# Batch 1's attention scores from float32 q and k as loaded, in a kernel of top-32 attention and two gated layers

## The chip, the cores and the metric

The kernel runs on one core of one Trainium2 chip. The metric is the device time of one execution in microseconds. Engine names in the profile: PE is TensorE's matmul, PEld its weight load, DVE is VectorE, ACT is ScalarE, POOL is GpSimd, SP is the engine from whose queue most DMAs are issued.

## The reference, cut to what matters

Three layers follow one another. The change lies in the first.

```python
# q, k, v: (4, 8, 576, 64) float32: 4 batches, 8 heads, 576 positions, 64 dims
scores = (1.0 / np.sqrt(D)) * np.matmul(q, k.transpose(0, 1, 3, 2))
kth = np.partition(scores, -32, axis=-1)[..., -32:-31]
scores = np.where(scores >= kth, scores, -1000000000.0)   # keep the 32 largest
attn = softmax(scores)
x = np.matmul(attn, v)                                    # -> (2304, 512)
x = (sigmoid(x @ w_gate) * (x @ w_val)) @ w_out           # d_ff 1536
# then: a noisy top-2 router over 8 experts, relu(x @ w1[e]) @ w2[e], weighted sum
```

Which 32 scores of a row are kept depends on their order, so the scores need more than float16's precision.

## The kernel before, in words

**Units.** Attention is cut into units of one batch `b`, one pair of heads `hp` (4 pairs) and one block of 128 query rows. 576 rows are four full blocks and one of 64 rows. A full unit has two tiles, one per head, of 128 queries by 576 keys; a half unit holds the 64 rows of both heads in one tile. So a batch has 16 full units with 32 tiles, and 4 half units with 4 tiles. q and k come transposed, with the two heads of a pair on rows (partitions) 0 to 63 and 64 to 127.

**Where q and k come from.** `kq_ops` (from L200) has two ways. With `first` true, k and q of a pair are loaded as float32 into a "khl" buffer (L213, L214), and the score matmul reads them there. With `first` false they are loaded into a staging tile "st" (L224, L225); ACT copies them times 64 to float16 (L235), POOL scales the original by 64 (L236) and subtracts the float16 part from it (L237), which leaves the low half; then SP copies the halves in eight strips into "khl" and "qs" (L232, L233), so that each head has its high and low half one above the other on 128 rows. Before, batch 0 goes the first way, batches 1 to 3 the second. There are 5 "khl" buffers and 3 "st" buffers; a pair of the second way takes two "st" while it is split, and keeps one until its strips are laid. The weights of the second layer pass through the same "st" buffers, ahead of these pairs.

**The score matmuls.** `qk` in `attention` has the same two ways. For batch 0, a tile is two float32 matmuls (288 keys each) on the 64 rows of its head (L336). For the others a tile is four float16 matmuls on all 128 rows, with high and low half of q against k's high halves, then k's low halves (L344); a half unit's are eight, on 64 columns of the array each (L347). One PSUM tile "ps" takes the scores; ACT copies it to SBUF (L352) before the next tile may be written. The scale of the exponent (`SC`) and a factor that the cut-off search uses (`facs`) differ between the two ways, since the second way's scores are 64 x 64 times as large.

**After the scores.** DVE finds each row's largest values (L361 to L370), ACT and POOL a lower bound of the cut-off (L396 to L402), DVE the exact cut-off (L409) and the mask (L424); ACT takes the exponent (L379). PE transposes the masked rows (L453 to L473), ACT copies them out (L460 to L480), and PE multiplies them with v (L494). The transposes, the product with v and the router's steps share three PSUM banks "tp". The products become the input of the second layer, `moe1` (L534, L573), which runs on PE by chunks of 128 or 256 rows whenever a chunk is ready; its end holds the router (its logits are read by DVE at L637, L638). The experts (L804, L830) come last.

**What sets the order.** Each operation is given to a small planner (`Plan`) with an engine, a duration as an estimate, a priority and the buffers that it takes. The planner plays the schedule through and emits the instructions of every engine in the order in which they start there. On the chip each engine's queue is in that order. Attention's priority is ten times the unit's number; the loads of a batch's q and k have that of its units less 70. Operations of one engine that take the same kind of buffer keep the order in which they were made. A score operation is told to take 0.9 us in batch 0 and 0.5 us in the others.

Of the kernel before, what the change touches and what calls it, by code (L numbers as in the profile page):

```python
# [17 lines left out]
OP = mybir.AluOpType  # L18
PSUM = bass.MemoryType.PSUM

B, H, S, D = 4, 8, 576, 64
# [7 lines left out]
SQ, SX, SG, SV, SO, SX2, S1, S2 = 2.0 ** 6, 2.0 ** 6, 2.0 ** 4, 2.0 ** 5, 2.0 ** 6, 2.0 ** 7, 2.0 ** 6, 2.0 ** 6  # L29
# [4 lines left out]

CUT = 1.75 + 2.0 ** -23, 1.75

SC = [1.0 / 8.0] + [1.0 / (8.0 * SQ * SQ)] * (B - 1)
SW = S + 8
TILES = B * 36
LOD = 4, 1  # L40
# [8 lines left out]
class Plan:  # L49
# [10 lines left out]
    def op(self, eng, dur, prio, fn, deps=(), alloc=(), use=(), lat=None, chain="", dma=False):  # L60
        o = Unit()
        o.eng, o.dur, o.prio, o.fn, o.lat = eng, dur, prio, fn, LAT[eng] if lat is None else lat
        o.alloc, o.use, o.next, o.same = list(alloc), list(alloc) + list(use), [], []
        o.n, o.id, o.dma = 0, len(self.ops), dma
        deps = list(deps)
        for t in {h.tag for h in o.alloc}:
            deps.append(self.last.get((eng, chain, t)))
            self.last[eng, chain, t] = o
        for d in deps:
            if d is not None:  # L70
                (d.same if d.eng == eng and not d.dma else d.next).append(o)
                o.n += 1
        for h in o.use:
            h.left += 1
        self.ops.append(o)
        return o
# [51 lines left out]
def attention_moe_kernel(ctx: ExitStack, tc: tile.TileContext, qT, kT, v, w_gate, w_val, w_out,  # L128
# [3 lines left out]
    V, A, P, G = nc.vector, nc.scalar, nc.tensor, nc.gpsimd  # L132
# [25 lines left out]
    facs = const.tile([128, 2, 2], FT, name="facs")  # L158
    G.memset(facs, CUT[1])
    for b in range(2):  # L160
        G.memset(facs[:, b, 0:1], -SC[b])
    NB = (REG - CAP) // BLK
    nbi = const.tile([1, E + 2], I32, name="nbi")
    ohsum = const.tile([128, E], FH, name="ohsum")
# [15 lines left out]
    def layers(fast):  # L180
# [12 lines left out]
        op = plan.op  # L193

        def tile_of(tag, shape, dt, name=None):
            pool = psum if tag in ("ps", "tp", "mm") else stage if tag == "st" else work
            return pool.tile(shape, dt, name=name or tag, bufs=CAPS[tag])
# [112 lines left out]
        def attention(u, kqr, prio):  # L310
# [16 lines left out]
            for t in R:  # L327
                hp_ = plan.tile("ps")

                def qk(t=t):  # L330
                    T[t].ps = tile_of("ps", [128, 2, 512], FT)
                    if u.b == 0:
                        for j in range(2):
                            for s in (t,) if u.nt == 2 else range(2):
                                d = slice(64 * s, 64 * s + 64)
                                P.matmul(T[t].ps[:, j, :288] if u.nt == 2 else T[t].ps[d, j, :288], kqr.kq[d, 1, u.q0:u.q0 + n],  # L336
                                         kqr.kq[d, 0, j * 288:j * 288 + 288], start=True, stop=True)
                        return
                    for c in range(2):
                        for j in range(2):  # L340
                            o = T[t].ps[:, j, :288]
                            ks = slice(j * 288, (j + 1) * 288)
                            if u.nt == 2:
                                P.matmul(o, kqr.qs[:, t, u.q0:u.q0 + 128], kqr.khl[:, c, t, ks], start=c == 0, stop=c == 1)  # L344
                            else:
                                for s in range(2):
                                    P.matmul(T[t].ps[64 * s:64 * s + 64, j, :288], kqr.qs[:, s, 512:576],  # L347
                                             kqr.khl[:, c, s, ks], start=c == 0, stop=c == 1)

                def cp(t=t):  # L350
                    T[t].s = tile_of("sS", [128, S], FT)
                    A.activation(T[t].s.rearrange("p (j n) -> p j n", j=2), T[t].ps[:, :, :288], AF.Copy)  # L352
                a = op("PE", 0.5 if u.b else 0.9, prio, qk, kqr.done, alloc=[hp_], use=[kqr.h])
                cps.append(op("ACT", 0.54, prio, cp, [a], alloc=[T[t].hs], use=[hp_]))

            def chunks(t):
# [7 lines left out]
            def top(rounds, src, tmp, first):  # L364
# [6 lines left out]
                if not fast:  # L371
                    for t in R:
                        V.tensor_copy(good[:, TILES + 6 - u.i - t:TILES + 7 - u.i - t], T[t].m[:, 31:32])
                    V.tensor_scalar(u.m[:, :, 32], u.m[:, :, 0], -SC[u.b], None, op0=OP.mult)

            def ex(t):
                def f():
                    T[t].e = tile_of("e", [128, S], FT)
                    A.activation(T[t].e, T[t].s, AF.Exp, bias=T[t].m[:, CM:CM + 1], scale=SC[u.b])  # L379
                return f  # L380

            if fast:
                c1 = []
                for t in R:
                    c1.append(op("DVE", 1.16, prio, chunks(t), c1 + [cps[t]], alloc=[] if t else [u.hm], use=[T[t].hs]))
                c2 = op("DVE", 1.62 if u.nt == 2 else 1.45, prio, lambda: top(3, lambda t: T[t].cand, lambda t: T[t].cand, 0), c1)
                c2 = op("POOL", 0.15, prio - 1, lambda: G.tensor_tensor(  # L387
                    u.m[:, :, 24:26], u.m[:, :, 0:24:23], facs[:, min(u.b, 1), None, :].to_broadcast([128, u.nt, 2]), op=OP.mult),
                    [c2], use=[u.hm])
                ys = []  # L390
                for t in R:
                    hg = plan.tile("sg")

                    def sg(t=t):
                        T[t].sg = tile_of("sg", [128, S], BF)
                        A.activation(T[t].sg, T[t].s, AF.Sign, scale=-CUT[0], bias=T[t].m[:, 25:26],  # L396
                                     accum_out=T[t].m[:, 26:27])

                    def y(t=t):
                        T[t].y = tile_of("y", [128, SW], FT)  # L400
                        G.tensor_scalar(T[t].y[:, S:], places, T[t].m[:, 26:27], NEG, op0=OP.add, op1=OP.mult)
                        G.tensor_tensor(T[t].y[:, :S], T[t].s, T[t].sg, op=OP.mult)  # L402
                    a = op("ACT", 0.78, prio, sg, [c2], alloc=[hg], use=[T[t].hs])
                    ys.append(op("POOL", 1.4, prio, y, [a], alloc=[T[t].hy], use=[hg, T[t].hs]))
                exs = [op("ACT", 0.68, prio + 0.5, ex(t), [c2], alloc=[T[t].he], use=[T[t].hs]) for t in R]

                def rank():
                    for t in R:
                        V.max(good[:, TILES - 1 - u.i - t:TILES + 7 - u.i - t], T[t].y)  # L409
                r4 = op("DVE", 0.68 * u.nt, prio, rank, ys + ranks[-1:], use=[T[t].hy for t in R])  # L410
            else:
                def whole():
                    alloc_m()
                    for t in R:
                        T[t].y = tile_of("y", [128, SW], FT)[:, :S]
                    top(4, lambda t: T[t].s, lambda t: T[t].y, 0)
                r4 = op("DVE", 4.9 * u.nt, prio, whole, cps, alloc=[u.hm] + [T[t].hy for t in R], use=[T[t].hs for t in R])
                exs = [op("ACT", 0.68, prio + 0.5, ex(t), [r4], alloc=[T[t].he], use=[T[t].hs]) for t in R]
# [43 lines left out]
            for t in R:  # L462
                ht = plan.tile("tp")
                a = op("PE", 0.44, prio, tr(t), [mk[t], ch.open], alloc=[ht], use=[T[t].he])
                evs.append(op("ACT", 0.5, prio, ev(t), [a] + evs[-1:], alloc=[hpt] if t == 0 else [],
                              use=[ht] + ([hpt] if t else [])))
# [7 lines left out]
            a = op("PE", 0.11 * u.nt + 0.11, prio, tr5, mk + [iv, ch.open], alloc=[h5], use=[T[t].he for t in R] + [hpx])  # L474
# [13 lines left out]
            def av():  # L488
                u.po = tile_of("tp", [128, n], FT)
                for kb in range(NK):  # L490
# [5 lines left out]
            a = op("PE", 1.31 if u.nt == 2 else 0.78, prio, av, evs + [VB[u.b, kb][2] for kb in range(NK)],  # L496
                   alloc=[hav], use=[hpt] + [VB[u.b, kb][0] for kb in range(NK)])
# [10 lines left out]
            a = op("DVE", 0.22, prio - 1, times, [a], use=[hav, hpx])  # L508
# [379 lines left out]
        i = 0  # L888
        for b in range(B):
# [3 lines left out]
            for qt in range(5) if b < B - 1 else (4, 0, 1, 2, 3):  # L893
# [11 lines left out]
                for hp in range(4):  # L905
                    u = Unit()
# [6 lines left out]
        KQ = {(0, 0): kq_ops(0, 0, -10, True)}  # L913
# [27 lines left out]
        if fast:  # L941
            a = op("SP", 5.0, 26, load_small)
# [18 lines left out]
        late = [r for u in [u for u in units if u.ends][-2:] for r in u.ch.rows]  # L961
        for i, u in enumerate(units):
            if (u.b, u.hp) not in KQ:
                KQ[u.b, u.hp] = kq_ops(u.b, u.hp, 10 * i - 70, False)
            if (u.b, 0) not in VB:
                for kb in range(NK):
                    v_ops(u.b, kb, 10 * i - 20)
            attention(u, KQ[u.b, u.hp], 10 * i)
            if (u.b, u.q0, u.hp) == (1, 128, 0):
                init_out(10 * i)  # L970
            if u.ends:
                moe1(u.ch, 10 * i + PM)
                if len(routers) == ends - 2:
                    raise_counts(0, 512)
                    early = list(entered)
# [83 lines left out]
```

## Time and profile before

| | us |
|---|---|
| median of 3 runs | 1325.57 (1324.25 to 1325.79) |
| the profiled execution | 1323.6 |
| its span, first to last instruction | 1321.9 |
| PE busy | 1228.2 |
| DVE busy | 869.1 |
| ACT busy | 791.6 |
| POOL busy | 740.9 |

The mean granted TensorE clock is 0.955 of full speed. Batch 1's scores are the matmuls of L344 and L347 between 246 and 415 us of the span.

Busy time is the union of an engine's instructions, and matmuls overlap in it: one may start before the one ahead has left the array. What a group of matmuls takes of PE's time is read from its start to the start of what follows it without a wait.

### The profile page before, as it was taken

Reading aid. Unit: us, or ns where it says so; the run is one execution under the profiler, and the core shown is the slowest. Engines: PE = TensorE matmul, PEld = TensorE weight load, DVE = VectorE, ACT = ScalarE, POOL = GpSimd, SP = SyncE. Lnnn points to the kernel's source line nnn. Section 1 sums busy time; section 2 is a strip of 40 time slices with the busy share of each in tenths; the row PEclk is TensorE's granted clock in tenths of the full one; section 3 lists DMA queues with packets and bytes.
Section 4 is the critical chain, followed back from the end, with each engine's and each line's share of the span. In section 5 each row is a group of like instructions: output and inputs, shape, how many; then the busy total and the mean of one; then the engine's idle time right before and its main releaser. Section 6 shows DMA issues by size and latency. Waiting matters only on the chain. (4 is left out here: it accounts for less than half of the span.)

```text
span 1321.9 us, 29643 instructions
## 1 busy us (share of the span) xinstructions
PE 1228.2 (93%) x10669; PEld 896.4 (68%) x10670; DVE 869.1 (66%) x3608; ACT 791.6 (60%) x1788; POOL 740.9 (56%) x1005
## 2 busy tenths in 40 slices
PE   5578799799999999999999999999999999999997
PEld 3347466586776867886777876877666666676674
DVE  6999889998799887888789875455114324233111
ACT  5777678787777877786787774565224324333221
POOL 5989887787476786666676654442222322222221
PEclk9558899899999899999999999999999999999999
DMA  7434331342004310014100003167547576575441
GB/s 222 115 108 122 124 106 27 100 133 112 17 2 101 87 47 10 11 36 121 53 2 2 18 9 97 50 185 204 99 73 194 122 159 171 102 189 132 77 72 22
DMA packets 104463, 119.93 MB, mean 91 GB/s; under 512 B 56561, under 2 KB 65905, under 8 KB 104306
## 3 DMA queue, kind: packets, MB, share of 16 engines
q1 hardware_dynamic: 94194, 97.97, 27.1%
q0 software_dynamic: 10112, 19.97, 8.2%
q8 instruction: 86, 1.41, 0.5%
q14 instruction: 71, 0.58, 0.2%
HBM read 77.22 MB, written 20.63 MB: 74 GB/s over the span
## 5 line engine op out<-in xcount | busy, mean ns | idle before, releaser
L534 PEld LDWEIGHTS <-w 128*128 128x128 f16 x3456 | 276.9, 100 | 38.0 <-issue 12.9
L534 PE MATMUL mm<-xch,w 128*128 128x256 f16 (+1 forms) x2880 | 285.9, 256 | 7.4 <-ACT th L541 3.7
L812 DVE SCALAR_TENSOR_TENSOR g<-mm,g 128x256 f16<-128x256 f32 (+1 forms) x192 | 72.0, 379 | 243.6 <-ACT g L809 233.1
L402 POOL TENSOR_TENSOR y<-sS,sg 128x576 f32<-128x576 f32 x144 | 194.9, 1354 | 9.1
L804 PE MATMUL mm<-xch,w 128*128 128x256 f16 (+1 forms) x2016 | 190.3, 255 | 0.0
L804 PEld LDWEIGHTS <-w 128*128 128x128 f16 x2016 | 170.2, 98 | 23.5
L361 DVE MAX8 cand<-sS 128x8 f32<-128x72 f32 x1152 | 166.8, 217 | 20.6 <-ACT sS L352 20.2
L830 PEld LDWEIGHTS <-g 128*128 128x128 f16 x960 | 92.8, 98 | 106.3 <-DVE g L812 3.4
L573 PE MATMUL mm<-w,g 128*128 128x512 f16 x648 | 158.2, 389 | 1.0 <-POOL w L281 0.7
L424 DVE SCALAR_TENSOR_TENSOR e<-sS,good,e 128x576 f32<-128x576 f32 x144 | 155.5, 1099 | 2.3 <-ACT e L379 1.5
L786 POOL DMA_INDIRECT v<-xd,ids x40 | 47.0, 1175 | 163.5 <-DVE ws L776 155.1
L842 POOL DMA_INDIRECT out<-e,ids x40 | 63.8, 1595 | 131.3 <-ACT e L839 58.6
L809 ACT ACTIVATE g<-mm 128x256 f16<-128x256 f32 (+1 forms) x192 | 65.8, 346 | 112.6 <-PE mm L804 106.6
L551 POOL TENSOR_TENSOR g<-th,g 128x128 f16<-128x128 f32 (+1 forms) x144 | 93.5, 653 | 68.8 <-ACT g L548 65.7
L409 DVE MAX8 good<-y 128x8 f32<-128x584 f32 x144 | 109.9, 763 | 25.8 <-POOL y L402 21.0
L396 ACT ACTIVATE sg<-sS,m 128x576 bf16<-128x576 f32 x144 | 110.7, 770 | 23.5 <-POOL m L387 22.6
L494 PE MATMUL tp<-pt,v 128*64 128x128 f32 (+3 forms) x1600 | 116.9, 285 | 7.0 <-ACT e L379 5.1
L830 PE MATMUL tp<-w,g 128*128 128x512 f16 x504 | 115.6, 379 | 1.7 <-DVE g L812 1.6
L494 PEld LDWEIGHTS tp<-pt,v 128*64 128x64 f32 (+1 forms) x1600 | 85.2, 143 | 41.5 <-issue 23.5
L573 PEld LDWEIGHTS <-g 128*128 128x128 f16 x648 | 63.6, 100 | 67.6 <-issue 9.2
L453 PE MATMUL tp<-ident,e 128*128 128x128 f32 x576 | 91.6, 296 | 17.2 <-DVE e L424 15.7
L379 ACT ACTIVATE e<-sS,m 128x576 f32<-128x576 f32 x144 | 106.5, 768 | 0.2
(160 smaller groups left out, 2073.7 us busy)
## 6 DMA issues: line engine op xcount, KB each, us to landing
st<-w SPq DMA_DIRECT2D x64, 512.0 KB
khl<-st SPq DMA_DIRECT2D x48, 144.0 KB
st<-w_gate SPq DMA_DIRECT2D x12, 512.0 KB
st<-w_val SPq DMA_DIRECT2D x12, 512.0 KB
st<-w_out SPq DMA_DIRECT2D x12, 512.0 KB
out<-x SPq DMA_DIRECT2D x6, 768.0 KB
v<-v_s SPq DMA_DIRECT2D x16, 256.0 KB
xd<-y SPq DMA_DIRECT2D x16, 256.0 KB
```

The lines of the kernel that those rows point to most:

```text
L361: V.max(T[t].cand[:, 8 * c:8 * c + 8], T[t].s[:, 72 * c:72 * c + 72])
L379: A.activation(T[t].e, T[t].s, AF.Exp, bias=T[t].m[:, CM:CM + 1], scale=SC[u.b])
L396: A.activation(T[t].sg, T[t].s, AF.Sign, scale=-CUT[0], bias=T[t].m[:, 25:26], accum_out=T[t].m[:, 26:27])
L402: G.tensor_tensor(T[t].y[:, :S], T[t].s, T[t].sg, op=OP.mult)
L409: V.max(good[:, TILES - 1 - u.i - t:TILES + 7 - u.i - t], T[t].y)
L424: return lambda: V.scalar_tensor_tensor(T[t].e, T[t].s, good[:, TILES + 6 - u.i - t:TILES + 7 - u.i - t], T[t].e, op0=OP.is_ge, op1=OP.mul ...
L494: P.matmul(u.po[64 * s:64 * s + 64, :], VB[u.b, kb][1][:k, (2 * u.hp + s) * D:(2 * u.hp + s + 1) * D], rhs, start=kb == 0, stop=kb == NK - 1)
L534: P.matmul(r.ps[:, a, :], wt.t[:, a, c, kb, fo:fo + 128], ch.x[x][:, kb, :], start=i == 0, stop=i == 11)
L551: G.tensor_tensor(r.g[:, 1], r.th, r.g[:, 0], op=OP.subtract)
L573: P.matmul(r.ps, g[:, c, 128 * t:128 * t + 128], WO[f // 4].t[:, d, f % 4, :], start=f == 0 and i == 0, stop=f == 11 and i == 2)
L804: P.matmul(r.ps, W[kb].w[c][:, 0, f * 128:f * 128 + 128], q.x[:, 4 * x + kb, :], start=i == 0, stop=i == 11)
L830: P.matmul(r.ps, gs[f].g[:, c, 128 * t:128 * t + 128], W[4 + f // 2].w[d][:, f % 2, :], start=f == 0 and i == 0, stop=f == 7 and i == 2)
```

## The change

Batch 1's scores go the first way, as batch 0's: q and k are loaded as float32 and used as they are. Batches 2 and 3 stay as they were. The scale and the factor follow, and so does the planner's estimate.

```diff
-SC = [1.0 / 8.0] + [1.0 / (8.0 * SQ * SQ)] * (B - 1)
+SC = [1.0 / 8.0] * 2 + [1.0 / (8.0 * SQ * SQ)] * 2
...
     for b in range(2):
-        G.memset(facs[:, b, 0:1], -SC[b])
+        G.memset(facs[:, b, 0:1], -SC[2 * b])
...
-                    if u.b == 0:
+                    if u.b < 2:
                         for j in range(2):
...
-                a = op("PE", 0.5 if u.b else 0.9, prio, qk, kqr.done, alloc=[hp_], use=[kqr.h])
+                a = op("PE", 0.5 if u.b > 1 else 0.9, prio, qk, kqr.done, alloc=[hp_], use=[kqr.h])
...
-                    u.m[:, :, 24:26], u.m[:, :, 0:24:23], facs[:, min(u.b, 1), None, :].to_broadcast([128, u.nt, 2]), op=OP.mult),
+                    u.m[:, :, 24:26], u.m[:, :, 0:24:23], facs[:, u.b // 2, None, :].to_broadcast([128, u.nt, 2]), op=OP.mult),
...
-                KQ[u.b, u.hp] = kq_ops(u.b, u.hp, 10 * i - 70, False)
+                KQ[u.b, u.hp] = kq_ops(u.b, u.hp, 10 * i - 70, u.b < 2)
```

## Rows read from the trace of the kernel before

**Rows 1.** The page's busy times: engine, busy us, share, instructions.
```profile
PE 1228.2 (93%) x10669; PEld 896.4 (68%) x10670; DVE 869.1 (66%) x3608; ACT 791.6 (60%) x1788; POOL 740.9 (56%) x1005
```

**Rows 2.** Busy us (instructions) by stretch; granted clock, DMA share, GB/s last.
```profile
0.00:100.00 100.00, 63.39 (x222) 37.44 (x224) 85.75 (x297) 67.34 (x132) 79.54 (x104) 0.70 0.49 147
...
180.00:260.00 80.00, 66.90 (x583) 47.60 (x584) 72.78 (x337) 62.15 (x140) 61.38 (x90) 0.89 0.29 76
260.00:440.00 180.00, 172.11 (x1511) 130.92 (x1509) 159.15 (x766) 137.13 (x317) 131.92 (x203) 0.98 0.25 76
440.00:820.00 380.00, 372.64 (x3650) 289.83 (x3649) 315.99 (x1574) 282.71 (x678) 253.85 (x405) 1.00 0.14 40
```

**Rows 3.** Instructions on tile ps: count, ns min/median/max, first and last start.
```profile
L344 PE MATMUL ps<-khl,qs x384: 282/286/444, 246.2 to 788.4; 128*128 128x288 f16 x192
...
L336 PE MATMUL ps<-khl x160: 402/507/847, 4.5 to 243.4; 64*128 64x288 f32 x128, 64*64 64x288 f32 x32
...
L347 PE MATMUL ps<-khl,qs x96: 286/286/310, 401.6 to 630.9; 128*64 128x288 f16 x96
```

**Rows 4.** PE's timeline around float32 scores: start, length, line, operands, count.
```profile
211.19 1.23 PE L336 MATMUL ps<-khl 64*128 64x288 f32 x4
212.36 1.51 PE L534 MATMUL mm<-xch,w 128*128 128x128 f16 x24
...
216.38 0.38 PE L473 MATMUL tp<-ident,e 128*64 128x128 f32 x2
216.69 1.23 PE L336 MATMUL ps<-khl 64*128 64x288 f32 x4
```

**Rows 5.** PE's timeline around float16 scores.
```profile
285.89 0.65 PE L344 MATMUL ps<-khl,qs 128*128 128x288 f16 x4
286.38 2.78 PE L534 MATMUL mm<-xch,w 128*128 128x256 f16 x24
...
293.81 0.38 PE L473 MATMUL tp<-ident,e 128*64 128x128 f32 x2
294.03 1.47 PE L534 MATMUL mm<-xch,w 128*128 128x256 f16 x12
```

**Rows 6.** PE's timeline at a float32 half unit of batch 0.
```profile
225.43 1.19 PE L336 MATMUL ps<-khl 64*64 64x288 f32 x8 [1.07 <-ACT sS L352]
226.55 1.46 PE L494 MATMUL tp<-pt,v 128*64 128x128 f32 x20
```

**Rows 7.** PE's timeline at the last float16 half unit of batch 1.
```profile
414.09 0.68 PE L347 MATMUL ps<-khl,qs 128*64 128x288 f16 x8
414.71 1.48 PE L534 MATMUL mm<-xch,w 128*128 128x256 f16 x12
```

**Rows 8.** POOL's subtraction for the halves: count, ns min/median/max, first and last start.
```profile
L237 POOL TENSOR_TENSOR st<-st x12: 2361/2378/2936, 183.3 to 604.2; 128x1152 f16<-128x1152 f32 x12
```

**Rows 9.** POOL's timeline, one of these subtractions.
```profile
230.43 2.37 POOL L237 TENSOR_TENSOR st<-st 128x1152 f16<-128x1152 f32 x1
```

**Rows 10.** DVE's timeline beside it.
```profile
230.49 2.92 DVE L424 SCALAR_TENSOR_TENSOR e<-sS,good,e 128x576 f32<-128x576 f32 x1
...
236.43 0.16 DVE L638 TENSOR_TENSOR sp<-sp,tp 128x8 f32<-128x8 f32 x1
```

**Rows 11.** The masks on DVE: count, ns min/median/max, first and last start.
```profile
L424 DVE SCALAR_TENSOR_TENSOR e<-sS,good,e x144: 798/819/2918, 20.7 to 834.0; 128x576 f32<-128x576 f32 x144
```

**Rows 12.** PE's timeline, the next matmul after that: in brackets the wait.
```profile
236.74 2.60 PE L494 MATMUL tp<-pt,v 128*64 128x128 f32 x20 [5.13 <-ACT e L379]
```

**Rows 13.** ACT's last copy ahead of that matmul, in the timeline of all engines.
```profile
232.95 0.26 ACT L480 ACTIVATE px<-tp 128x128 f32<-128x128 f32 x1
```

**Rows 14.** PE's busy us and granted clock in a stretch.
```profile
234.00:240.00 6.00, 3.26 (x24) 0.50 0.66 151
```

**Rows 15.** PE's waits behind the first and the third score group of batch 1.
```profile
249.12 0.33 PE L471 MATMUL tp<-ident,px 128*128 128x128 f32 x1 [2.27 <-DVE cand L370]
...
253.19 0.33 PE L471 MATMUL tp<-ident,px 128*128 128x128 f32 x1 [0.57 <-POOL px L443]
```

## Prediction

> **What bounds the kernel now.** I read the page's busy times first, then a table of busy time by stage, then the PE timeline of the two kinds of score matmul, then the waits and the DVE and POOL timelines around the largest PE stall. The page says that PE is busy for 93% of the span [rows 1]. The table says where it is not [rows 2]: in the first 100 us PE works 63.39 us, in 180 to 260 us (the end of batch 0's attention and the start of batch 1's) 66.90 of 80, in 260 to 440 us 172.11 of 180, in 440 to 820 us 372.64 of 380. So before about 260 us the attention steps on DVE (72.78 of 80 busy) set the pace and PE has holes; after it PE is the bound. What is not done in a hole is done later, so the end moves by what PE's work grows, less what its holes shrink.
>
> **Where the change falls.** Only batch 1 changes. Its scores ran from 246 us [rows 3] to 415 us [rows 7]: nearly all in the stage in which PE is the bound. That decides the sign for me.
>
> **Scores on PE, full tiles.** A full unit has two score tiles (one per head). Before, a tile is four float16 matmuls on all 128 rows; 384 of them stand for batches 1 to 3 [rows 3], so batch 1 has 128, or 32 tiles. After, a tile is two float32 matmuls, which the trace of batch 0 shows as four instructions on 64 rows. From the start of a group of four to the start of what follows without a wait:
> - float32: 212.36 - 211.19 = 1.17 us [rows 4];
> - float16: 286.38 - 285.89 = 0.49 us [rows 5].
> That is 0.68 us more. The entry costs too: after the pair of L473 the float32 group starts 216.69 - 216.38 = 0.31 us later [rows 4], a 128-row matmul 294.03 - 293.81 = 0.22 us later [rows 5]: 0.09 us. So 0.77 us a tile, and 32 x 0.77 = 24.6 us.
>
> The bounds: within a float32 group the four starts are closer than the group is long. Its 1.23 us [rows 4] hold three steps and one duration; with the median duration of 0.51 us [rows 3] a step is 0.24 us and four are 0.96, that is 0.47 over float16: 32 x 0.47 = 15.0 us if the edges of the group were hidden. I take 0.77, because it is what the rows show to the instruction behind; 15.0 and 24.6 are the ends.
> The rule that bears on this stands in the Trainium skill, "TensorEngine Tiling (Array Packing)", section "Key Properties": changing the tiling mode, not just the tile, drains TensorE. By that rule the edges can't be hidden, since the neighbours are 128-row matmuls, and the trace agrees (1.17 against 0.96); it gives 24.6, without it the sum would be 15.0.
>
> **Scores on PE, the half tiles.** The last 64 rows of batch 1 have four units. Before, eight float16 matmuls on 64 columns (96 for three batches [rows 3]): 414.71 - 414.09 = 0.62 us [rows 7]. After, eight float32 instructions on 64x64: 226.55 - 225.43 = 1.12 us [rows 6]. Four x 0.50 = 2.0 us. Both change the mode at the edges. PE's work grows by 24.6 + 2.0 = 26.6 us (17.0 at the low end).
>
> **What is removed.** For each of batch 1's four head pairs: an ACT copy to float16, a POOL scaling, a POOL subtraction of 2.38 us [rows 8], eight strip copies on SP's queue and the staging tiles. POOL's own time is worth nothing: no PE wait is on it. But DVE pays for the subtraction. At 230.43 it starts and takes 2.37 us [rows 9]; the mask on DVE that starts at 230.49 takes 2.92 us [rows 10] where its median is 0.82 [rows 11]: 2.1 us lost. The Trainium skill, "SBUF — State Buffer", section "Who interferes with whom", calls this an exclusive lock between DVE and GpSimd, and holds it for the whole instruction; the trace agrees for this mask, which ends 0.6 us behind the subtraction.
>
> Here that loss reached PE. PE waits 5.13 us once, from 231.6 to 236.7 us [rows 12]; the row names ACT, but the last of ACT's copies that this step reads had ended at 233.2 [rows 13]. The attention-times-v step writes a PSUM bank of the three that the router's logits also use, and DVE reads those last at 236.43 [rows 10], in order behind the slow mask. And PE's clock was granted at 0.50, the 1.2 GHz level, in 234 to 240 us [rows 14], after PE had stood still. If batch 1's subtraction is not there, 2.1 us of the wait go. Of the 6 us at the low level half was lost (3.0 us); I count half of that again, 1.5 us, as not certain. After the stall goes, the next in line are the router's own DVE steps.
>
> I don't count four such gains. The splits of batch 2 are chained behind batch 1's for the staging tiles "st" alone, so they move up: two of them (three tiles, two per pair in work, one held until its strips are laid) take the places that batch 1's first two had, and the third runs when the first is laid. What is fewer is some three splits in 225 to 300 us, and behind 260 us DVE is not what PE waits for: all PE idle of 260 to 440 us is 7.9 us [rows 2].
>
> **What the holes swallow.** The first batch 1 scores fall where PE waits anyway: 2.27 us behind the first and 0.57 us behind the third [rows 15]. The longer tiles fill 0.77 + 0.57 = 1.3 us of it, unless what PE waits for starts later for them.
>
> **Moved.** Pair 0 of batch 1 finds the fifth "khl" buffer free and is loaded at the start instead of at 170 us: two DMAs, 0.59 MB. At the 147 GB/s of that stage [rows 2] this is 4.0 us of DMA time, and the weight loads queued behind it on SP are late by up to that. DVE, which is busy 85.75 of the first 100 us, hides it: 0, at most 4.0. The other three pairs' loads wait on SP for a buffer of batch 0, as their strips did before, with two DMAs behind the wait instead of eight; the x writes and v loads queued behind it on SP gain, and PE waits for neither: 0. New factors, scales and their index: same instructions, 0. The planner is told 0.9 instead of 0.5 us, so the queues' order changes; that is a gain or a loss for which no row stands, and I bound it by one stall like the one above: 5.1 + 3.0 = 8.1 us either way, taken as 0.
>
> **Sum.** 26.6 - 2.1 - 1.5 - 1.3 = +21.7 us. On the profiled execution's 1323.6 us (span 1321.9 and 1.7 around it) that gives 1345.3; the median of the runs shown lies 2.0 us above that execution, so **1347**.
>
> **Rivals.**
> - **A, faster: DVE is freed and all holes close.** Place: 180 to 440 us. Idle there is 13.1 + 7.9 = 21.0 us [rows 2]. The granted clock of 0.89 over 80 us means 17.6 us at the low level, half lost, 8.8; 0.98 over 180 us likewise 3.6. Together 33.4 us: 26.6 - 33.4 = -6.8, 1319. It decides from 26.6 us recovered on. For it: the one stall shown hangs on a split. Against it: three splits of batch 2 run in the same stretch, and only that stall (6.6 us with its clock) has this cause in the rows.
> - **B, no change: the two heads run side by side.** They lie on rows 0 to 63 and 64 to 127. If they overlapped, two tiles would take 1.26 against 0.98 us: 16 x 0.28 = 4.5, + 2.0 - 4.9 = +1.6, 1327. The Trainium skill's same section says that tiles run matmuls in parallel. Against it: there is one score tile in PSUM, so head 1 waits for ACT's copy of head 0, and the rows show groups of four with other work between them [rows 4].
> - **C, worse: the new order makes another stall** of 8.1 us and the old one stays (3.6 us back): 1347 + 11.7 = 1359. For it: 0.4 us a tile is what the planner believes, 0.77 is what PE takes, so PE runs late on its plan.
> - **D, cheaper tiles:** 17.0 - 4.9 = +12.1, 1338.
>
> **Chances.** Forecast 0.66 (its own range 1339 to 1356), C 0.15, D 0.05, A 0.09, B 0.05. About 0.2% (2.7 us) is what a measurement of this kernel can tell from no change. Slower: forecast, C and D, 0.86; same: B, 0.05; faster: A, 0.09. The range leaves out A, B and the far part of C: 1330 to 1359.
>
> **What would show it.** In the changed trace: L336 with twice its instructions and 1.17 us to the next start; PE busy up by about 20 to 27 us; PE idle of 260 to 440 us still under 10 us; eight L237 instead of twelve; the 5.1 us stall shorter or gone. It is wrong if PE's busy time hardly grows, or if PE's idle time in 180 to 440 us falls from 21 us to under 5.

## The result, and the profile after

| | kernel before | changed kernel | ratio, 95% interval |
|---|---|---|---|
| first comparison | 1325.21 us | 1341.97 us (1337.91 to 1345.53) | 1.0126 (1.0089 to 1.0163) |
| second comparison (run a1_again) | 1324.10 us | 1337.93 us (1335.70 to 1341.85) | 1.0113 (1.0093 to 1.0134) |

The change makes the kernel slower: by 16.8 and 13.8 us between the medians, by 17 and 15 us by the ratios, whose intervals run from 12 to 22 us. 1347 was forecast, with 1330 to 1359 as the range. The profiled execution is the first comparison's slowest, 1345.53 us; the sum that started from the profiled execution before gave 1345.3.

The page of the changed kernel, to be read beside [rows 1]: PE's busy time rose by 22.0 us, and the span by 21.9. (In the profiled execution of a1_again, which is the same kernel, PE's busy time is 1242.1 us, 13.9 above the kernel before, and the span is 1334.0; the last section comes back to this.)

```profile
span 1343.8 us, 29515 instructions
...
PE 1250.2 (93%) x10669; PEld 902.4 (67%) x10670; DVE 862.4 (64%) x3608; ACT 789.6 (59%) x1784; POOL 728.4 (54%) x997
```

PE's idle time as a whole is the same, 93.6 against 93.7 us, but it lies elsewhere. The same table of stages as [rows 2] (PE, PEld, DVE, ACT, POOL busy, granted clock, DMA share, GB/s), first a row of the kernel before that [rows 2] leaves out, then the changed kernel's:

```profile
100.00:180.00 80.00, 64.56 (x595) 47.15 (x593) 70.34 (x216) 57.09 (x133) 72.57 (x81) 0.85 0.37 116
...
100.00:180.00 80.00, 61.64 (x545) 44.95 (x544) 73.17 (x224) 60.34 (x136) 77.93 (x82) 0.81 0.34 112
180.00:260.00 80.00, 72.55 (x603) 50.27 (x601) 72.14 (x353) 61.99 (x144) 58.40 (x93) 0.91 0.19 56
260.00:440.00 180.00, 178.66 (x1453) 128.84 (x1451) 147.32 (x734) 128.59 (x304) 112.84 (x189) 1.00 0.19 59
440.00:820.00 380.00, 367.90 (x3582) 286.60 (x3581) 312.74 (x1564) 279.99 (x670) 249.52 (x396) 1.00 0.13 36
```

In 180 to 440 us PE idles 7.5 + 1.3 = 8.8 us where it idled 21.0; in 260 to 440 us it has almost no room left. DVE does less there (147.32 against 159.15 us of 180). In 100 to 180 us PE idles 18.4 us against 15.4, in 440 to 820 us 12.1 against 7.4. (The stretches are cut by time, so they don't hold the same work in both kernels.) ACT's copies of the scores now wait for PE, as the page's group of L352 shows (busy, mean ns of one, idle ahead of it and what ended most of that). They wait 26.4 us for L336 and 9.3 for L344; before, it was 12.4 and 3.7:

```profile
L352 ACT ACTIVATE sS<-ps 128x576 f32<-128x576 f32 x144 | 92.9, 645 | 36.0 <-PE ps L336 26.4
```

PE's timeline around three score groups of batch 1, to be read beside [rows 4 and 5]:

```profile
305.26 1.24 PE L336 MATMUL ps<-khl 64*128 64x288 f32 x4
306.42 1.09 PE L453 MATMUL tp<-ident,e 128*128 128x128 f32 x8
307.35 1.47 PE L534 MATMUL mm<-xch,w 128*128 128x256 f16 x12
308.76 1.23 PE L336 MATMUL ps<-khl 64*128 64x288 f32 x4
...
405.01 1.19 PE L336 MATMUL ps<-khl 64*64 64x288 f32 x8
406.13 1.48 PE L534 MATMUL mm<-xch,w 128*128 128x256 f16 x12
```

A full tile takes 306.42 - 305.26 = 1.16 us to the next start, a half unit 1.12. The entry shows too: twelve matmuls of L534 take 308.76 - 307.35 = 1.41 us ahead of a score group. In the kernel before, the same twelve take 295.34 - 294.03 = 1.31 us ahead of a float16 group ([rows 5] has their start):

```profile
295.34 0.65 PE L344 MATMUL ps<-khl,qs 128*128 128x288 f16 x4
```

The large stall is gone. POOL's subtractions are eight instead of twelve, and in 225 to 260 us there is none. DVE's masks at that place take 0.80 us, about their median, and DVE reads the router's logits at 234.60, 1.8 us earlier than before:

```profile
230.21 0.80 DVE L424 SCALAR_TENSOR_TENSOR e<-sS,good,e 128x576 f32<-128x576 f32 x1
...
234.60 0.16 DVE L638 TENSOR_TENSOR sp<-sp,tp 128x8 f32<-128x8 f32 x1
```

and PE's waits of 180 to 260 us (total, times, longest) hold nothing over 1.3 us:

```profile
PE ps L336 <- ACT sS L352: 4.7, 5, 1.3
```

### The profile page after: what moved, and what is told of

Read it like the earlier page. It is cut to its first block, busy times and chain, and to the rows that moved or that the text cites. A ratio compares the mean times of both kernels' runs of the same rounds, so it can differ in the third digit from the quotient of the medians.

```text
span 1343.8 us, 29515 instructions
## 1 busy us (share of the span) xinstructions
PE 1250.2 (93%) x10669; PEld 902.4 (67%) x10670; DVE 862.4 (64%) x3608; ACT 789.6 (59%) x1784; POOL 728.4 (54%) x997
## 3 DMA queue, kind: packets, MB, share of 16 engines
q8 instruction: 86, 1.41, 0.4%
## 5 line engine op out<-in xcount | busy, mean ns | idle before, releaser
L534 PEld LDWEIGHTS <-w 128*128 128x128 f16 x3456 | 274.1, 100 | 41.5 <-issue 16.6
L534 PE MATMUL mm<-xch,w 128*128 128x256 f16 (+1 forms) x2880 | 282.0, 254 | 6.8 <-DVE th L544 4.9
L361 DVE MAX8 cand<-sS 128x8 f32<-128x72 f32 x1152 | 166.7, 217 | 25.6 <-ACT sS L352 25.2
L424 DVE SCALAR_TENSOR_TENSOR e<-sS,good,e 128x576 f32<-128x576 f32 x144 | 150.4, 1066 | 3.8 <-ACT e L379 2.8
L336 PE MATMUL ps<-khl 64*128 64x288 f32 (+1 forms) x320 | 108.9, 497 | 37.1 <-ACT sS L352 31.2
L396 ACT ACTIVATE sg<-sS,m 128x576 bf16<-128x576 f32 x144 | 110.4, 769 | 18.4 <-POOL m L387 18.1
L352 ACT ACTIVATE sS<-ps 128x576 f32<-128x576 f32 x144 | 92.9, 645 | 36.0 <-PE ps L336 26.4
```

The lines of the kernel that those rows point to most:

```text
L361: V.max(T[t].cand[:, 8 * c:8 * c + 8], T[t].s[:, 72 * c:72 * c + 72])
L424: return lambda: V.scalar_tensor_tensor(T[t].e, T[t].s, good[:, TILES + 6 - u.i - t:TILES + 7 - u.i - t], T[t].e, op0=OP.is_ge, op1=OP.mul ...
L534: P.matmul(r.ps[:, a, :], wt.t[:, a, c, kb, fo:fo + 128], ch.x[x][:, kb, :], start=i == 0, stop=i == 11)
```

## The experiments

Each was timed in five rounds beside the kernel before; a ratio is to that. E1, e4 and e6 give the planner the same operations and durations as the changed kernel, so they keep its order and change what PE pays for batch 1's tiles (and, in e4 and e6, how a pair's q and k are loaded: four and five DMAs instead of two). The traces bear it out: PE's work has the same sequence in the changed kernel, e1 and e4, score groups counted as one, and so have DVE's and ACT's.

**e1_one_pass.** The changed kernel with batch 1's tile as two bfloat16 instructions. It leaves out the lower 16 bits of q and k, so it shows a price and is no kernel to use.

```diff
+ kq = (upper 16 bits of each float32 of kqr.kq, as bfloat16) if u.b == 1 else kqr.kq
- P.matmul(..., kqr.kq[d, 1, u.q0:u.q0 + n], kqr.kq[d, 0, j * 288:j * 288 + 288], ...)
+ P.matmul(..., kq[d, 1, u.q0:u.q0 + n], kq[d, 0, j * 288:j * 288 + 288], ...)
```

> The changed kernel, but batch 1's score matmuls read only the upper 16 bits of each float32 q and k (as bfloat16, same 64 rows, same tiles, same order of everything), so one pass instead of float32's; the scores of batch 1 are coarser for it. My theory (the end moves by PE's time in the score groups): a group has two instructions instead of four and each is shorter; with the step of 0.12 us that four float16 matmuls show (0.49/4) and the same edges it is about 0.55 us from entry to the next start instead of 1.26, so 32 x 0.71 + 4 x 0.5 = 25 us less than the changed kernel: about 1317, which is 8 us below the kernel before. Rival 1 (the planner's new order makes the loss): the order is the changed kernel's, so it stays near 1342. Rival 2 (PE's work is the whole loss, and the missing splits give nothing): about 1325.

Measured: 1321.68 us, ratio 0.9985 (0.9968 to 1.0001). The tile takes 302.68 - 302.33 = 0.35 us to the next start:

```profile
302.33 0.43 PE L338 MATMUL ps<-khl 64*128 64x288 bf16 x2
302.68 1.46 PE L496 MATMUL tp<-pt,v 128*64 128x128 f32 x20
```

The changed kernel's order is refuted as the loss by itself: with the same order and cheaper tiles the loss is gone. But of the work taken out, 32 x 0.82 + 4 x 0.75 = 29 us, only some 16 to 20 us came off the time. Part of the rest is idle time again: in 260 to 440 us PE idles 180 - 171.51 = 8.5 us here, where the changed kernel has 1.3:

```profile
260.00:440.00 180.00, 171.51 (x1513) 124.64 (x1513) 154.36 (x777) 140.83 (x334) 120.82 (x199) 0.99 0.26 79
```

**e4_two_row_groups.** Each head's q on both halves of the rows, k by halves of the keys.

```diff
+ for j in range(2):
+     d = slice(64 * j, 64 * j + 64)
+     nc.sync.dma_start(r.kd[d], kT[b, hp].rearrange("(c p) s -> p c s", c=2)[:, :, 288 * j:288 * j + 288])
+     nc.sync.dma_start(r.qd[d], qT[b, hp].rearrange("(c p) s -> p c s", c=2))
...
+ P.matmul(T[t].ps[:, j, :288], kqr.qd[d, s, u.q0:u.q0 + n], kqr.kd[d, s], start=True, stop=True)
```

> The changed kernel, but for batch 1 each head's q is loaded on both halves of the 128 rows and its k by halves of the keys, so that the two float32 matmuls of a tile (288 keys each) lie on different 64 rows and write different PSUM banks; four loads a pair instead of two. My theory: if the two row groups overlap as those of the half units do (eight instructions in 1.12 us against four in 1.17), a tile takes about 0.7 us to the next start instead of 1.17, and the half units somewhat less too: 32 x 0.47 + 2 = 17 us less than the changed kernel, about 1325. If the groups don't overlap: 1342. Rival 1 (order): 1342 too, since the planner's numbers are the same.

Measured: 1325.68 us, ratio 1.0000 (0.9987 to 1.0013), as forecast. Four float32 instructions of the same shape take 301.04 - 300.36 = 0.68 us when they lie on two row groups:

```profile
300.36 0.76 PE L344 MATMUL ps<-qs,khl 64*128 64x288 f32 x4
301.04 1.47 PE L588 MATMUL mm<-w,g 128*128 128x512 f16 x6
```

**e6_full_rows.** All 128 rows, q of the other head replaced by zeros.

```diff
+ nc.sync.dma_start(r.qz[d, s], qT[b, hp, d])
+ nc.sync.dma_start(r.qz[o, s], zeros)            # o: the other head's 64 rows
...
+ P.matmul(T[t].ps[:, j, :288], kqr.qz[:, s, u.q0:u.q0 + n], kqr.kf[:, j * 288:j * 288 + 288], start=True, stop=True)
```

> The changed kernel, but batch 1's float32 matmuls use all 128 rows: k of both heads as it is loaded, q of one head with zeros on the other head's rows (filled by two more DMAs a head pair). Four instructions a tile as in the changed kernel, in the same order, but no change of the array's tiling at their edges. My theory (the edges cost 0.29 us a tile): four steps of 0.24 us, 0.97 us to the next start and no longer entry, so 32 x 0.29 = 9 us less than the changed kernel, about 1333. Rival (the edges are hidden in the array, and float32's passes are the price): 1342.

Measured: 1331.41 us, ratio 1.0063 (1.0041 to 1.0085), against 1.0113 for the changed kernel in the same comparison: 6.6 us less. In front of a 128-row matmul the group takes 301.95 - 300.98 = 0.97 us, in front of one on 64 columns 305.93 - 304.87 = 1.06:

```profile
300.98 1.14 PE L346 MATMUL ps<-qs,khl 128*128 128x288 f32 x4
301.95 1.46 PE L590 MATMUL mm<-w,g 128*128 128x512 f16 x6
...
304.87 1.13 PE L346 MATMUL ps<-qs,khl 128*128 128x288 f32 x4
305.93 1.46 PE L511 MATMUL tp<-pt,v 128*64 128x128 f32 x20
```

So the edges of a 64-row group are a price of their own: against 1.16 to 1.17 us and 0.09 to 0.10 of entry it is 0.2 to 0.3 us a tile. This is what the rule on changing the tiling mode in the Trainium skill ("TensorEngine Tiling (Array Packing)", "Key Properties") leads one to expect, and e4 agrees with the same section's statement that tiles run matmuls in parallel.

**e12_twice.** The kernel before, its order and splits kept, with PE's work raised.

```diff
-                    for c in range(2):
+                    for c in (0, 1) * (2 if u.b == 1 else 1):
```

> The kernel before in its own order, splits and all, the planner still told 0.5 us, but each score group of batch 1 is computed twice, the second time over the first: eight float16 matmuls a tile instead of four. PE's work grows by 32 x 0.49 + 4 x 0.61 = 18.1 us, the order and the splits don't change. My theory (PE's work in this stretch moves the end, less what holes swallow): 13 to 18 us above the kernel before, 1338 to 1343. Rival (the changed kernel's loss is its order; work alone is swallowed by PE's holes of 180 to 440 us): under 8 us above, 1332 or less.

Measured: 1337.14 us, ratio 1.0100 (1.0083 to 1.0116), that is +13.2 us (11.0 to 15.4) for 18.1 us of work: 0.73 of it (0.61 to 0.85) reaches the end. The time lies 0.9 us below the range that I had given, and well above the rival's 1332. PE idles 2.6 us in 260 to 440 us where [rows 2] has 7.9:

```profile
260.00:440.00 180.00, 177.42 (x1605) 136.60 (x1603) 151.48 (x730) 131.06 (x300) 122.21 (x190) 1.00 0.23 69
```

**e2_order_only, e11_order_more, e7_true_price.** Only the planner's number for batch 1's scores changes, in the kernel before (0.9, then 1.26) and in the changed kernel (1.26).

```diff
- op("PE", 0.5 if u.b else 0.9, prio, qk, ...)               # kernel before
+ op("PE", 0.5 if u.b > 1 else 0.9, prio, qk, ...)           # e2
+ op("PE", (0.9, 1.26, 0.5, 0.5)[u.b], prio, qk, ...)        # e11; e7: the same line in the changed kernel
```

> The kernel before, with one number changed: the planner is told 0.9 us instead of 0.5 for batch 1's scores, which stay float16. My theory: only the order changes, 1325 with up to 8 us either way. Rival 1 (order makes the loss): 1335 to 1342.

Measured: 1321.91 us, ratio 0.9972 (0.9962 to 0.9983): 3.7 us faster. An order planned with 0.9 us is no loss by itself. It is not the changed kernel's own order, which has no splits of batch 1 to place; that one is held in e1, e4 and e6.

> The kernel before, float16 scores, with the planner told 1.26 us for batch 1's scores. e2 told it 0.9 and came out 3 us below the kernel before. If a longer estimate as such is good for the order: 1319 to 1322, below e2. If an order's gain is chance of a few us: anything from 1319 to 1330.

Measured: 1338.83 us, ratio 1.0109 (1.0094 to 1.0124): 14.4 us slower, outside both expectations. A longer estimate is not good as such, and an order is worth more than the few us that I had taken as its bound. Among PE's waits of 180 to 440 us the longest is:

```profile
PE tp L494 <- DVE sp L638: 4.9, 1, 4.9
```

This is the wait of [rows 12] once more, and here the profile names DVE's L638, which confirms how that row was read.

> The changed kernel, with the planner told 1.26 us for batch 1's scores, what a tile takes of PE in the trace, instead of 0.9. My theory (PE's work is the loss, the order moves the end by a few us): 1335 to 1343, against 1338 for the changed kernel in the last comparison. Rival 1 (the plan's error of 0.36 us a tile makes the loss): 1330 or less.

Measured: 1339.39 us, ratio 1.0115 (1.0100 to 1.0130), as the changed kernel, though PE's order is another one. Telling the planner the true price repairs nothing.

**e3_idle_splits.** The changed kernel with batch 1's splits as idle work.

```diff
+ a = op("SP", 1.6, prio, again, alloc=[hs, hl], lat=3.0)      # k and q once more, into st
+ a = op("ACT", 1.06, prio, ...)                               # the three split operations, as before
+ a = op("POOL", 1.15, prio, ...)
+ op("POOL", 2.35, prio, ...)
```

> The changed kernel, with batch 1's splits put back as idle work: q and k are loaded once more into st tiles, ACT, POOL and POOL work on them as before, and nobody reads the result (no strips are laid). My theory: POOL's subtractions hold up DVE again and PE's holes of 180 to 260 us come back in part: 2 to 6 us above the changed kernel, 1344 to 1348. Rival 2 (the missing splits give nothing): 1342. Rival 3 (they give most of 12 us, what PE's idle time of 180 to 440 us fell by): 1350 or more.

Measured: 1348.26 us, ratio 1.0165 (1.0142 to 1.0188): by the ratios 5 to 7 us above the changed kernel. Since added operations also give a new order, and e11 shows what an order can do, this is no price of the splits; it does not show that they cost the 12 us by which the holes of 180 to 440 us shrank. But the wait for the router's logits is back (L652 is L638 of the other kernels):

```profile
PE tp L485 <- DVE sp L652: 3.6, 1, 3.6
```

Just ahead of it two masks take 1.61 and 1.68 us, while POOL works on a split's scaling and other operations. In e1, e4 and e6, which run without these splits, PE has no such wait; in e2, e11 and e12, which have them, it lasts 5.1, 4.9 and 3.7 us. E9 has them in an order of its own and has not this wait, but one of 6.4 us for a mask; so the order has a part in where a stall falls.

**e8_two_groups_b01, e5_two_groups_all, e9_two_groups_b0.** e4's layout for batches 0 and 1, for all four, and for batch 0 alone (the kernel before with batch 1 in halves, the planner told e2's number). All three have orders of their own.

```diff
- if b == 1:      # e4
+ if b < 2:       # e8; e5: b < 4; e9: b == 0
```

> As e4, but batch 0 as well as batch 1 has each head's q and k on both halves of the rows, and the planner is told 0.7 us for both. PE's score groups of batch 0 shrink by 0.48 us a tile (15 us at full clock). PE has holes in that stage, so my theory gives back only a part: 1318 to 1325. If the holes of batch 0 are as deep as DVE's pace makes them, 1325 as in e4.

Measured: 1321.27 us, ratio 0.9979 (0.9966 to 0.9992). It is faster than both kernels, by 3 and by about 17 us.

> All four batches from float32 with both halves of the rows, the planner told 0.7 us, no splits at all. Against e8: 64 tiles more at 0.78 instead of 0.49 us, +18.6 us of PE work where PE is the bound, less the splits of two batches, which e3 prices at 6 us a batch in a stage where PE has holes and my theory at 0 to 2 us a batch behind it. My theory: 12 to 18 us above e8, 1332 to 1342. Rival (the splits cost 6 us a batch everywhere): about 6 us above e8, 1328.

Measured: 1335.79 us, ratio 1.0097 (1.0078 to 1.0117): 14.5 us above e8, inside what I expected, and far from the rival's 6. It fits PE's work as the price, and splits of batches 2 and 3 that give little back; but the order is new as well, so this does not show it.

> The kernel before, batch 1 in float16 halves, with batch 0 on both halves of the rows as in e8, and the planner told 0.7 us for batch 0 and 0.9 for batch 1 (e2's number). Against e8, batch 1's 32 tiles fall from 0.78 to 0.49 us (9 us) and its splits come back (6 us by e3): 3 us below e8, about 1318.

Measured: 1334.72 us, ratio 1.0077 (1.0064 to 1.0090), where I expected 1318. PE's busy time fell to 1204.4 us, by 23.8, and its idle time grew by 31.7 to 125.4. The cheaper work of batch 0 did not shorten the kernel, and PE's holes grew; which part of that is the order was not told apart.

**a1_again.** The changed kernel once more; its times stand in the table above.

> The changed kernel as it is, once more, since its four runs lie between 1337.9 and 1345.5. Both theories: 1342, and an interval of its ratio to before that is narrower than 1.0089 to 1.0163. With the kernel before in a new order at -3 (e2) and the splits at -6 (e3), the work of 26.6 us would leave +17.

## Why the prediction was right

**The sign and its place.** Right: batch 1's scores fall where PE is the bound. With the order held, the time follows PE's price of a tile (to the next start, and 0.09 us of entry where the tiling changes): 0.44 us in e1 gives 1321.7, 0.78 in e4 1325.7, 1.0 in e6 1331.4, 1.26 in the changed kernel 1338 to 1342. The place is shown too. Up to 230 us the profiled executions of a1_again and e4 lie within 2 us of each other, matmul by matmul; the last score instructions of batch 1 start at 412.0 and 398.1 us, 13.9 us apart; and at the end the spans are 1334.0 and 1321.1, 12.9 apart. E1 has 394.5 and 1319.5.

```profile
L336 PE MATMUL ps<-khl x320: 402/403/847, 4.7 to 412.0; 64*128 64x288 f32 x128, 64*64 64x288 f32 x32
...
L344 PE MATMUL ps<-qs,khl x160: 402/403/507, 234.1 to 398.1; 64*128 64x288 f32 x128, 64*64 64x288 f32 x32
```

**The work on PE.** Right: 1.16 to 1.17 us, 0.09 to 0.10 of entry, 1.12 us for a half unit, so 26.6 us. That the edges can't be hidden was the choice between 15.0 and 24.6 us; e6, where they are gone and 6.6 us come back, shows it.

**The stall of 5.1 us.** Right in its cause: the mask behind it is short again, the wait is gone, and with the idle splits of e3 it is back. The size was taken too small: 2.1 us of it were counted, and all 5.1 went, in an order that also puts other work at that place. More masks paid than this one: in the kernel before, all eight that start while a subtraction runs take 1.65 to 2.92 us, against the median of 0.82, while DVE's max8 of L361 takes 0.22 us beside a subtraction as elsewhere. The 1.5 us for the clock stay open: in 240 to 250 us the first profiled execution was granted 0.57 and the second 1.00.

**Where the splits go.** Right as far as the trace shows it: batch 2's first two take the places of batch 1's first two (their subtractions start at 183.9 and 203.8 us, where batch 1's started at 183.3 and 209.4), and in 225 to 300 us one is left of four. One sentence was too wide: that no PE wait is on POOL. [rows 15] have one of 0.57 us, but it is on a copy (L443) and not on a split.

**What was mis-sized.** The forecast was +21.7, the measured loss is 15 to 17 us by the ratios. The term that is too small is "what the holes swallow": it was 1.3 us, from two waits ahead of 260 us. By e12, 0.27 of work added in this stage is swallowed, which is an estimate of 7 us of 26.6. The sum gave nothing for PE's idle time of 260 to 440 us, and that fell from 7.9 to 1.3 us. Its two largest waits before, to be set against the one that is left in the changed kernel:

```profile
PE ps L344 <- ACT sS L352: 3.0, 4, 1.8
PE mm L534 <- ACT th L541: 1.7, 1, 1.7
...
PE mm L534 <- ACT th L541: 1.3, 2, 1.0
```

So holes closed that don't lie behind the first scores: 1.8 us of the first row stand ahead of a score group at 344 us, the 1.7 us at 276. The other gains were put at 3.6 us. Read from e1 and e4, a tile at float16's 0.49 us would give about 1322.3 in the changed kernel's order without splits, that is 2.7 us below the kernel before: order and splits together. As an estimate, 26.6 - 7 - 2.7 = 17. How the 2.7 us divide stays open, since no run changes the splits and keeps the order.

**The order.** Taken as 0 with a bound of 8.1 us either way. What the changed kernel's own order cost or gave was not measured apart from the splits; together they are near 0, by the estimate above. The bound did not hold: e2 is at -3.7, e11 at +14.4 us, with the same work. That the forecast came near was luck in this term, and rival C was priced too low.

**The rivals.** A asked for 26.6 us to come back; 12.2 us of holes closed in 180 to 440 us, and 7.7 us opened in 100 to 180 and 440 to 820 us. B needed the heads side by side, which did not happen; e4 gives up the heads and sets the key halves side by side, and lands at 1325.7, near the 1327 of B. C asked for a new stall of 8.1 us, and no wait of PE between 180 and 820 us is longer than 2.6. D's time is the one that came nearest, 1338 against 1341.97 and 1337.93, but not its mechanism: the tiles cost 1.16 us and not 0.96, and the holes swallowed more. So the number alone would not have told D from the forecast.

## What to carry to other kernels

Price a matmul group from its start to the start of what follows, with its entry, and not by its length or by PE's busy time; then ask whether PE has holes where it runs. On 64 rows, lay two independent matmuls on the two row groups before paying for float32: four instructions of the same shape took 0.68 instead of 1.16 us. Where a planner orders the queues, test a change in more than one order, because orders of the same work lay 18 us apart.

## What the runs showed of the hardware that was not expected

Two profiled executions of the same changed kernel, the first comparison's and a1_again's, have spans of 1343.8 and 1334.0 us. PE's instructions have the same order in both, and the mean granted clock is 0.958 and 0.973 of full speed. In 230 to 240 us PE was busy for only 6.4 us in both. Then the first was granted 0.57 in 240 to 250 and 0.75 in 250 to 260 us, a mixture of the levels of 1.2 and 2.4 GHz; the second was granted 1.00, the upper level:

```profile
180.00:260.00 80.00, 71.42 (x645) 50.03 (x643) 74.89 (x375) 63.74 (x150) 60.76 (x97) 1.00 0.19 56
```

The same score group takes 2.29 us in the first and 1.24 in the second, and the next twelve matmuls of L534 start 252.88 - 247.77 = 5.1 us apart. The first execution's two rows, then the second's:

```profile
241.65 2.29 PE L336 MATMUL ps<-khl 64*128 64x288 f32 x4
252.88 2.56 PE L534 MATMUL mm<-xch,w 128*128 128x256 f16 x12
...
241.66 1.24 PE L336 MATMUL ps<-khl 64*128 64x288 f32 x4
247.77 1.65 PE L534 MATMUL mm<-xch,w 128*128 128x256 f16 x12
```

That is half of the 9.8 us. Nearly all of the other half opens behind 800 us; from 820 us on both were granted 0.99 on the mean, so its cause is not shown. Nor does a run's time follow its mean clock: 1344.89 us had 0.972 and 1339.06 us had 0.963. So a sum that is made against one execution, as this one was, carries the course of that execution with it: 1345.3 against 1345.53 us is closer than the forecast was good.
